# Rows of x in SBUF in bfloat16, DMA transposes in layers 2 to 4, a three-operation feature map and a new PSUM layout in a four-layer linear-attention and MLP kernel

## The chip, the cores and the metric

The kernel runs on one core of one Trainium2 chip. The metric is the device time of one execution in microseconds. A profile is one execution seen by the hardware profiler. TensorE multiplies matrices and writes PSUM; ScalarE (ACT), VectorE (DVE) and GpSimd (POOL) do elementwise work; SyncE (SP) issues DMAs. Each engine works through its own instructions in a fixed order and waits on semaphores for the others.

## What is computed

Four layers stand in a row: attention, MLP, attention, MLP, with the same weights in both turns. S = 2048 rows (tokens) of D = 576, 32 heads of 18, F = 4608. Weights and inputs are bfloat16.

```python
def _A_ref(x, wqkv, wo):                      # H = 32, Dh = 18
    q, k, v = split_heads(x @ wqkv)
    phi = lambda t: jnp.where(t > 0, t + 1, jnp.exp(t)) + 1e-6
    pq, pk = phi(q), phi(k)
    kv = jnp.einsum("bhsd,bhse->bhde", pk, v)
    z = jnp.einsum("bhsd->bhd", pk)
    num = jnp.einsum("bhqd,bhde->bhqe", pq, kv)
    den = jnp.einsum("bhqd,bhd->bhq", pq, z)[..., None] + 1e-6
    return merge_heads(num / den) @ wo

def _B_ref(x, w1, b1, w2, b2):
    y = _layernorm(x, axis=-1)
    h = _gelu(jnp.einsum("bsd,df->bsf", y, w1) + b1)
    return jnp.einsum("bsf,fd->bsd", h, w2) + b2

x = A_x
x = x + _A_ref(_layernorm(x, axis=-1), A_wqkv, A_wo)
x = x + _B_ref(_layernorm(x, axis=-1), B_w1, B_b1, B_w2, B_b2)
x = x + _A_ref(_layernorm(x, axis=-1), A_wqkv, A_wo)
x = x + _B_ref(_layernorm(x, axis=-1), B_w1, B_b1, B_w2, B_b2)
```

## The kernel before

**Tiles.** The 2048 rows are 16 row tiles of 128 and four chunks of 512 (four row tiles each). D = 576 is contracted in five blocks, four of 128 and one of 64. The heads are five groups: four of seven heads (126 columns) and one of four heads (72). The code numbers the layers from 0: layers 0 and 2 are attention ("A"), 1 and 3 the MLP ("B").

**The rows of x between layers** lie in a DRAM tensor `x_d` in float32. `residual` (line 329) adds a finished product in PSUM to the old row tile on VectorE (line 336) and stores the result to `x_d`; `prefetch_xo` (318) loads the old row tile back (in layer 0 from the input), and GpSimd adds the MLP's second bias to it (326). In layer 3 the result goes to the output.

**Layer norm** is a small pipeline, `LNPipe` (216). A row tile is fed to it and moves one stage on at every `tick` (228): a load of x where needed (237), statistics on VectorE (242 to 253), the inverse root by a power on GpSimd (258), the normalised tile into one of four buffers `y_ring` (274: GpSimd for tiles 2 to 15 of layer 0, VectorE mostly; 270: ScalarE for the first four tiles of an MLP), and the transpose: five TensorE transposes into PSUM (287), copied to `yT` by ScalarE (289) or VectorE (291). `yT` holds the transposed, normalised rows of all 16 tiles. In layer 0, `pre_a1_layer0` (642) feeds row tile t+4 and ticks ahead of step t; a tile needs four ticks to its transpose.

**An attention layer** is `layer_A` (344). Its first loop goes over the row tiles: `kv_proj(t)` (350: ten matmuls for k in two halves of 288 columns, ten for v), `kv_acc(t-1)` (375: five matmuls that add the products of v and the mapped k into `kvacc`, which stays in PSUM through the loop), and from t = 4 one `q_proj` (383: five matmuls of 512 columns, for one head group and one chunk). There are 20 of these; those left over are spread over what follows. The feature map `phi_from_psum` (307) is two ScalarE operations that read PSUM (exp, 309; x + 1 + 1e-6, 311) and two on VectorE in bfloat16 in SBUF (min and add, 312; max, 314). Then comes a set-up: the masked `kvacc` to SBUF (408, 412), `z` (418), `kv_wo` (427: kv times wo for a head group), `den_stage` (438: the denominators of a chunk, 20 small matmuls, four more that add 1e-6 by a row `eps_row` times a row of ones, a reciprocal and a masked copy on VectorE) and `scale_stage` (456: the reciprocal spread over a head group by one matmul, a ScalarE copy, and a product into the mapped q; the product is VectorE's, but GpSimd's for the last head group of chunks 1 to 3, 461 and 462). Then the output stage goes over the 16 row tiles: `wo_stage` (465, ten matmuls), its residual, the next chunk's `scale_stage`s, left-over `q_proj`s and `den_stage`s. In it the first four tiles are fed to the next MLP's norm.

**An MLP layer** is `LayerB` (521). For each chunk it runs nine groups of `m1_group` (529: four blocks of 128 hidden units, in pairs of matmuls of 64 rows that run side by side; ScalarE evicts with Gelu, 565; small ScalarE copies, 574, pass the turn on a PSUM bank), then for each row tile of the chunk the second matmul, 72 matmuls of 288 columns (616), and its residual. Meanwhile the next chunk's rows are fed to the norm (`feed_next`, 594), and in layer 1 the finished row tiles for layer 2.

**Order.** `pe` (136) chains TensorE's instructions into program order where it is on: in both MLP layers, in layer 2, and in layer 0 from row tile 8. Elsewhere, and on the other engines, the framework's scheduler orders by priority (program order) and by when it estimates that an instruction is ready. `chained` (128) keeps the loads in order on SP's queue.

**PSUM** has eight banks: three single ones (`ps_h`: k, q, z, den, rden, and two of four blocks of an MLP group), one for transposes (`ps_tp`), and two pairs (`ps_acc`, tags accA and accB: kvacc, v, kv_wo, wo, MLP).

Of the kernel before, what the change touches and what calls it, by code (L numbers as in the profile page):

```python
# [35 lines left out]
def build(tc, A_x, A_wqkv, A_wo, B_w1, B_b1, B_w2, B_b2, out, dbg=None, n_layers=4):  # L36
    nc = tc.nc
    dbg = dbg or {}
    with ExitStack() as ctx:
        const = ctx.enter_context(tc.tile_pool(name="const", bufs=1))  # L40
        ps_h = ctx.enter_context(tc.tile_pool(name="ps_h", bufs=3, space=PSUM))
        ps_tp = ctx.enter_context(tc.tile_pool(name="ps_tp", bufs=1, space=PSUM))
        ps_acc = ctx.enter_context(tc.tile_pool(name="ps_acc", bufs=1, space=PSUM))
        dpool = ctx.enter_context(tc.tile_pool(name="dram", bufs=1, space=DRAM))

        x_in = A_x.flatten_outer_dims()
        out_f = out.flatten_outer_dims()

# [15 lines left out]
        eps_row = const.tile([1, H], BF16, name="eps_row")  # L64
        one_row = const.tile([1, P], BF16, name="one_row")

        def build_masks(after):
            sel = nc.gpsimd.affine_select

            def fill(tile_, value):  # L70
# [10 lines left out]
            fill(eps_row, 1e-6)  # L81
            fill(one_row, 1.0)
# [6 lines left out]
                base=DH - 1, pattern=[[-126, G], [DH, H]], channel_multiplier=-1)  # L89
            fill(quad_mask, 1.0)  # L90
# [10 lines left out]
        wqkv_sb = const.tile([P, KD, 3 * D], BF16, name="wqkv_sb")  # L101
# [5 lines left out]
        b2_bc = const.tile([P, D], BF16, name="b2_bc")  # L107
        yT = const.tile([P, KD, S], BF16, name="yT")
        kvT = const.tile([P, G, 126], BF16, name="kvT")
        zsel = const.tile([P, G, H], BF16, name="zsel")  # L110
        NY = 4
        y_ring = [const.tile([P, DPAD], BF16, name=f"y_ring{i}") for i in range(NY)]
        NV = 3
        v_ring = [const.tile([P, G, P], BF16, name=f"v_ring{i}") for i in range(NV)]
        x_d = dpool.tile([NT, P, D], F32, name="x_d")

        work = ctx.enter_context(tc.tile_pool(name="work", bufs=2))
        blk = ctx.enter_context(tc.tile_pool(name="blk", bufs=NF))

        x0_tiles = {}  # L120

        NOSYNC = mybir.DependencyInfo(mybir.DependencyClass.NoSync, mybir.DependencyReason.SCHED_ONLY)
        SYNC = mybir.DependencyInfo(mybir.DependencyClass.Sync, mybir.DependencyReason.DATA)
        relay_sb = const.tile([P, 2], F32, name="relay_sb")
        nc.gpsimd.memset(relay_sb[:], 0.0)
        chain = dict(last=None)

        def chained(inst):
            if chain["last"] is not None:
                tc.add_manual_dep(inst.ins, chain["last"], NOSYNC, reason="start-up DMA issue order")  # L130
            chain["last"] = inst.ins.name
            return inst

        pe_chain = dict(on=False, last=None)

        def pe(inst):
            if pe_chain["on"]:
                if pe_chain["last"] is not None:
                    tc.add_manual_dep(inst.ins, pe_chain["last"], NOSYNC, reason="TensorE order in the MLP")
                pe_chain["last"] = inst.ins.name  # L140
            return inst

        def load_x0(t):
            x0 = blk.tile([P, D], BF16, name="x0", tag="blk")
            chained(nc.sync.dma_start(out=x0[:], in_=x_in[t * P:(t + 1) * P, :]))
            x0_tiles[t] = x0

        def load_wqkv(part):
            cols = slice(part * D, (part + 1) * D)
            chained(nc.sync.dma_start(out=wqkv_sb[:, 0:4, cols],  # L150
                                      in_=A_wqkv[0:4 * P, cols].rearrange("(k p) n -> p k n", p=P)))
            chained(nc.sync.dma_start(out=wqkv_sb[0:64, 4, cols], in_=A_wqkv[4 * P:D, cols]))

        load_x0(0)
        load_x0(1)
        load_wqkv(1)
        load_x0(2)
        load_x0(3)
        load_wqkv(2)
        load_x0(4)  # L160
        for i in (NY - 1, 0, 1, 2):
            nc.vector.memset(y_ring[i][:], 0.0)
        warm_ps = ps_h.tile([P, 512], F32, name="warm_ps", tag="h")
        for i in range(NWARM):
            nc.tensor.matmul(warm_ps[:], lhsT=y_ring[NY - 1][:, 0:P], rhs=y_ring[NY - 1][:, 0:512], start=True, stop=True)
        act_dummy = const.tile([P, 1], F32, name="act_dummy")
        nc.scalar.activation(out=act_dummy[:, 0:1], in_=neg_half[:, 0:1], func=ACT.Exp)
        nc.vector.memset(wqkv_sb[64:P, 4, :], 0.0)
        for vr in v_ring:
            nc.gpsimd.memset(vr[:, 4, 72:126], 0.0)  # L170
            nc.gpsimd.memset(vr[:, :, 126:127], 1.0)
            nc.gpsimd.memset(vr[:, :, 127:128], 0.0)

        def late_setup():
            build_masks(pool_last["norm"])
# [20 lines left out]
        def piece_b1_dma():  # L196
            b1_raw = work.tile([P, NF], BF16, name="b1_raw", bufs=1)
            with nc.allow_non_contiguous_dma(reason="tiny one-time bias transpose load"):
                chained(nc.sync.dma_start(out=b1_raw[:], in_=B_b1.rearrange("(f p) -> p f", p=P)))
            bias_stage["b1"] = b1_raw  # L200

        def piece_b2_dma():
            chained(nc.sync.dma_start(out=b2_bc[:], in_=B_b2.partition_broadcast(P)))

        def bias_casts():
            nc.vector.tensor_copy(out=b1T[:], in_=bias_stage.pop("b1")[:])

        late_pieces = [piece_wo, piece_b1_dma] + [(lambda i=i: piece_w1(i)) for i in range(9)] + \
                      [(lambda i=i: piece_w2(i)) for i in range(6)]
        late_pads = [late_setup]  # L210

        state = dict(ycnt=0, vcnt=0)
        pool_last = dict(norm=None)
        dve_last = dict(norm=None)

        class LNPipe:
# [3 lines left out]
            def feed(self, xt, t, kind, norm_eng, evac_eng="dve", load_from=None, after=None):  # L220
                self.items.append(dict(stage=(0 if load_from is None else -1), xt=xt, t=t, kind=kind,
                                       norm=norm_eng, evac=evac_eng, load=load_from,
                                       after=after))

            def busy(self):
                return len(self.items)

            def tick(self, transposes=1):
                for it in list(self.items):
                    st = it["stage"]  # L230
                    if st == 4:
                        if transposes == 0:
                            continue
                        transposes -= 1
                    if st == -1:
                        xn = work.tile([P, D], F32, name="xl", tag="xl", bufs=2)
                        nc.sync.dma_start(out=xn[:], in_=x_d[it["load"]])
                        it["xt"] = xn
                    elif st == 0:
                        xt = it["xt"]  # L240
                        stt = work.tile([P, 2, 6], F32, name="ln_st", bufs=4)
                        first = nc.vector.bn_stats(out=stt[:, 0, :], in_=xt[:, 0:HALF])
# [101 lines left out]
        def layer_A(li, next_kind, pre_a1=None):  # L344
# [49 lines left out]
            for t in range(NT):  # L394
                if t == NT // 2:
                    pe_chain["on"] = True
                if pre_a1 is not None:
                    pre_a1(t)
# [329 lines left out]
```

## Time and profile before

| what | us |
|---|---|
| median of 3 runs (lowest, highest) | 809.78 (809.3, 810.58) |
| the profiled execution, span | 809.3 |
| layer 0: to the end of the k/v loop, then set-up, then output stage | 74.6, 13.45, 35.89 |
| layer 1 (MLP) | 289.26 |
| layer 2: k/v loop, set-up, output stage | 55.49, 13.43, 38.26 |
| layer 3 (MLP) | 285.32 |
| after the last matmul | 3.60 |

The stages are cut where TensorE starts the first instruction of the next one. The granted TensorE clock was 0.996 over the span. These are the groups of instructions for the transposes, the feature map and the output stage (line, engine, operation, output and inputs, count, then busy time in us, mean ns of one, idle time of the engine just before them and what ended it):

```profile
L287 PE MATMUL tp<-ident,y_ring 128*128 128x128 bf16 x320 | 29.2, 223 | 3.5 <-DVE y_ring L274 2.5 <-POOL y_ring L274 0.6 <-POOL ln_rstd L258 0.3
L289 ACT COPY yT<-tp 128x640 bf16<-128x640 bf16 x24 | 16.7, 695 | 7.6 <-PE tp L287 7.6
L311 ACT ACTIVATE phi_a<-q_ps 126x512 bf16<-126x512 f32 (+1 forms) x40 | 23.7, 592 | 0.0
L336 DVE TENSOR_TENSOR xn<-m_ps,xo 128x576 f32<-128x576 f32 x16 | 12.1, 758 | 59.5 <-PE m_ps L616 59.5
L470 PE MATMUL wo_ps<-kvwo,pq 126*128 126x288 bf16 (+1 forms) x320 | 48.2, 298 | 13.5 <-POOL pq L462 10.2 <-DVE xn L336 2.1 <-ACT kvwo L434 0.5
```

Matmuls are pipelined, so a mean of one (223 ns for a transpose) is longer than the distance from one to the next.

### The profile page before, as it was taken

The numbers are of one execution on the slowest core, as the hardware profiler recorded it, in microseconds if no ns is written. First come the engines' busy times: TensorE is split into PE (matmuls) and PEld (weight loads), VectorE is DVE, ScalarE is ACT, GpSimd is POOL, SyncE is SP. The second block draws the span as 40 slices with busy tenths as digits, with TensorE's granted clock in tenths as the row PEclk, the third lists the DMA queues.
The fourth block names the chain that finished last, engine by engine and source line by source line (L and its number), as shares of the span: only waits on it lengthen the run. The fifth ranks groups of instructions, "written<-read, shape, count | busy, mean of one in ns | idle before, by whom it ended". The sixth has DMA issues, their size and how long they took to land.

```text
span 809.3 us, 16072 instructions
## 1 busy us (share of the span) xinstructions
PE 783.0 (97%) x6802; PEld 509.1 (63%) x6808; DVE 256.4 (32%) x714; ACT 348.8 (43%) x762; POOL 133.8 (17%) x186
## 2 busy tenths in 40 slices
PE   7999879999999999999999998899999999999998
PEld 4777554486468548745887765546854874685476
DVE  6775881034123403300344467431300300010000
ACT  4778745601630460065037786263047007404610
POOL 6981240012102201100100002120210110011000
PEclk9999999999999999999999999999999999999999
DMA  8991383011112200200110007711300120011000
GB/s 198 260 322 34 97 268 99 2 59 59 31 33 73 72 2 30 74 17 1 60 59 1 1 10 231 260 59 31 95 23 2 52 67 1 2 50 40 2 23 23
DMA packets 43649, 57.07 MB, mean 71 GB/s; under 512 B 10298, under 2 KB 28218, under 8 KB 43578
## 3 DMA queue, kind: packets, MB, share of 16 engines
q1 hardware_dynamic: 43578, 56.06, 22.9%
q8 instruction: 53, 0.87, 0.4%
q14 instruction: 18, 0.15, 0.1%
HBM read 39.53 MB, written 16.52 MB: 69 GB/s over the span
## 4 chain that ended last, share of the span: by engine, by line
PE 87%; POOL 4%; ACT 3%; DVE 2%; DMA 2%; issue 2%; SPq 0%; POOLq 0%; ACTq 0%; DVEq 0%
PE m_ps L616 35%; PE h_ps L569 19%; PE hp_ps L569 15%; PE q_ps L386 4%; PE k_ps L356 4%; PE wo_ps L470 3%; PE v_ps L367 2%; PE tp L287 2%; PE v_ps L364 2%; POOL y_ring L274 2%; ACT rden_bc L460 1%; PE kvacc L380 1%; POOL ln_rstd L258 1%; DMA wqkv_sb<-in_A_wqkv_dram 1%; DVE xn L336 1%
## 5 line engine op out<-in xcount | busy, mean ns | idle before, releaser
L616 PE MATMUL m_ps<-w_sb,hT 128*128 128x288 bf16 x2304 | 289.8, 286 | 0.0
L616 PEld LDWEIGHTS <-hT 128*128 128x128 bf16 x2304 | 223.2, 98 | 57.9 <-issue 3.4
L569 PEld LDWEIGHTS <-w_sb 64*128 64x128 bf16 x2304 | 124.5, 94 | 136.4 <-issue 1.9
L569 PE MATMUL hp_ps<-yT,w_sb 64*128 64x512 bf16 x1152 | 178.0, 376 | 0.0
L574 ACT COPY relay_sb<-relay_sb 128x1 f32<-128x1 f32 x144 | 28.5, 198 | 281.8 <-PE h_ps L569 239.2
L569 PE MATMUL h_ps<-yT,w_sb 64*128 64x512 bf16 x1152 | 147.9, 376 | 0.0
L565 ACT ACTIVATE hT<-h_ps,b1T 128x512 bf16<-128x512 f32 x144 | 91.0, 683 | 44.2 <-PE h_ps L569 44.2
L291 DVE COPY yT<-tp 128x640 bf16<-128x640 bf16 x40 | 19.6, 489 | 262.5 <-PE tp L287 262.5
L565 ACT ACTIVATE hT<-hp_ps,b1T 128x512 bf16<-128x512 f32 x144 | 91.1, 692 | 0.0
L258 POOL TENSOR_TENSOR ln_rstd<-ln_u,neg_half 128x1 f32<-128x1 f32 x64 | 35.5, 554 | 326.4 <-DVE ln_u L251 180.0
L326 POOL TENSOR_TENSOR xo<-xo,b_bc 128x576 f32<-128x576 f32 x32 | 40.9, 1278 | 181.9 <-DMA xo<-x_d 171.2
L470 PE MATMUL wo_ps<-kvwo,pq 126*128 126x288 bf16 (+1 forms) x320 | 48.2, 298 | 13.5 <-POOL pq L462 10.2
L569 PE MATMUL h_ps<-yT,w_tail 64*128 64x512 bf16 x144 | 54.1, 376 | 0.0
L569 PE MATMUL hp_ps<-yT,w_tail 64*128 64x512 bf16 x144 | 54.1, 376 | 0.0
L386 PE MATMUL q_ps<-yT,wqkv_sb 128*126 128x512 bf16 (+1 forms) x200 | 50.0, 382 | 0.5 <-ACT phi_a L311 0.5
L336 DVE TENSOR_TENSOR xbf<-m_ps,xo 128x576 bf16<-128x576 f32 x16 | 12.0, 752 | 117.4 <-PE m_ps L616 117.4
L470 PEld LDWEIGHTS <-pq 126*128 126x128 bf16 (+1 forms) x320 | 31.4, 101 | 27.9 <-POOL pq L462 11.7
L356 PE MATMUL k_ps<-wqkv_sb,yT 128*128 128x288 bf16 x320 | 45.7, 291 | 0.0
L309 ACT ACTIVATE phi_e<-k_ps 128x288 bf16<-128x288 f32 x64 | 27.2, 426 | 36.7 <-PE k_ps L356 36.7
L312 DVE TENSOR_SCALAR phi_e<-phi_e 128x288 bf16<-128x288 bf16 (+2 forms) x104 | 30.8, 297 | 31.1 <-ACT phi_e L309 30.9
L569 PEld LDWEIGHTS <-w_tail 64*128 64x128 bf16 x288 | 27.1, 94 | 17.1
L356 PEld LDWEIGHTS <-yT 128*128 128x128 bf16 x320 | 31.0, 99 | 9.3
(94 smaller groups left out, 656.0 us busy)
## 6 DMA issues: line engine op xcount, KB each, us to landing
x_d<-xn SPq DMA_DIRECT2D x48, 288.0 KB, 2.6
xo<-x_d SPq DMA_DIRECT2D x48, 288.0 KB, 3.0
xl<-x_d SPq DMA_DIRECT2D x24, 288.0 KB, 3.1
w_sb<-in_B_w_dram SPq DMA_DIRECT2D x6, 864.0 KB, 11.5
w_sb<-in_B_w_dram SPq DMA_DIRECT2D x9, 512.0 KB, 5.1
x<-in_A_x_dram SPq DMA_DIRECT2D x17, 144.0 KB, 5.3
xbf<-in_A_x_dram SPq DMA_DIRECT2D x16, 144.0 KB, 3.8
out_dram<-xbf SPq DMA_DIRECT2D x16, 144.0 KB, 1.7
```

The lines of the kernel that those rows point to most:

```text
L258: nc.gpsimd.tensor_tensor(out=rstd[:], in0=it["u"][:], in1=neg_half[:], op=ALU.pow)
L309: act_last["exp"] = nc.scalar.activation(out=e[0:rows, 0:n], in_=ps_ap, func=ACT.Exp).ins.name
L312: nc.vector.tensor_scalar(out=e[0:rows, 0:n], in0=e[0:rows, 0:n], scalar1=1.0, scalar2=1e-6, op0=ALU.min, op1=ALU.add)
L326: nc.gpsimd.tensor_tensor(out=xo[:], in0=xo[:], in1=b2_bc[:], op=ALU.add)
L336: nc.vector.tensor_tensor(out=xn[:].rearrange("p (h n) -> p h n", h=2), in0=halves, in1=xo[:].rearrange("p (h n) -> p h n", h=2), op=ALU.add)
L356: pe(nc.tensor.matmul(kp[:, 0:HALF], lhsT=yT[:, k, tok], rhs=wqkv_sb[:, k, D + half * HALF: D + (half + 1) * HALF], start=(k == 0), stop=( ...
L386: pe(nc.tensor.matmul(qp[0:GR[g], :], lhsT=wqkv_sb[:, k, GO[g]:GO[g] + GR[g]], rhs=yT[:, k, c * CA:(c + 1) * CA], start=(k == 0), stop=(k ...
L470: pe(nc.tensor.matmul(wp[:, half, 0:HALF], lhsT=pq[(g, c)][0:GR[g], j * P:(j + 1) * P], rhs=kvwo[g][0:GR[g], half * HALF:(half + 1) * HALF ...
L565: act_last["gelu"] = nc.scalar.activation(out=hT[f][:, 0:CB], in_=dst[n], func=ACT.Gelu_apprx_tanh, bias=b1T[:, f:f + 1], scale=1.0).ins.name
L569: mm = pe(nc.tensor.matmul(dst[n], lhsT=wt, rhs=mv, start=(seen[n] == 0), stop=(seen[n] == 8)))
L574: relay = nc.scalar.copy(out=relay_sb[:, 1:2], in_=relay_sb[:, 0:1])
L616: pe(nc.tensor.matmul(acc[:, half, 0:HALF], lhsT=hT[f][:, j * P:(j + 1) * P], rhs=w2_sb[:, f, half * HALF:(half + 1) * HALF], start=(f == ...
```

## The change

- **x in SBUF.** `x_sb` holds all rows in bfloat16. `x_d` and its stores and loads go; the input is loaded once, `residual` adds in place, and `bias_rows` makes x + b2 on GpSimd.
- **Norm.** `LNPipe` becomes `Norm`, with the steps `stats`, `rstd`, `norm` and `transposed`, and `Queue`, which takes every fed tile one step on at each tick. For layers 1 to 3 the transpose is a DMA from SBUF to SBUF on SP's queue. In layer 0 it stays on TensorE with a ScalarE copy; it is issued at the end of step t for row tile t+1.
- **Feature map.** exp on ScalarE, min and add on VectorE, then one VectorE operation that reads PSUM: max(x, 0) plus the former. For k all 576 columns go at once. The copy x + 1 on ScalarE goes.
- **PSUM.** Three pairs and two single banks. q, z, den, rden and layer 0's transposes share the two single banks; k, v, kvacc, kv_wo, wo and the MLP's second matmul share the pairs; the MLP's groups use two pairs, or one pair and the two single banks, in turn.
- **The small term 1e-6.** The weights of q lie in groups padded with zeros to 128 columns, so row 126 of a mapped q is one; `zsel` has 1e-6 there, and the four extra matmuls of `den_stage` go.
- **The rest.** All products of `scale_stage` are VectorE's. `pe` chains TensorE throughout. There are two buffers for v instead of three. The masks are built at row tile 8 of layer 0. The weights of q are loaded in ten DMAs, and b1 and b2 after w1.

```diff
-        ps_h = ctx.enter_context(tc.tile_pool(name="ps_h", bufs=3, space=PSUM))
-        ps_tp = ctx.enter_context(tc.tile_pool(name="ps_tp", bufs=1, space=PSUM))
-        ps_acc = ctx.enter_context(tc.tile_pool(name="ps_acc", bufs=1, space=PSUM))
-        dpool = ctx.enter_context(tc.tile_pool(name="dram", bufs=1, space=DRAM))
+        ps_pair = ctx.enter_context(tc.tile_pool(name="ps_pair", bufs=3, space=PSUM))
+        ps_one = ctx.enter_context(tc.tile_pool(name="ps_one", bufs=2, space=PSUM))
...
+            fill(zsel, 0.0)
+            sel(out=zsel[:, 0, :], in_=zsel[:, 0, :], compare_op=ALU.not_equal, fill=1e-6,
+                base=-126, pattern=[[0, H]], channel_multiplier=1)
...
+        def load_wq(k):
+            rows = P if k < 4 else 64
+            src = A_wqkv[k * P:k * P + rows, :]
+            chained(nc.sync.dma_start(out=wq_sb[0:rows, k, 0:4, 0:126],
+                                      in_=src[:, 0:504].rearrange("p (g c) -> p g c", g=4)))
+            chained(nc.sync.dma_start(out=wq_sb[0:rows, k, 4, 0:72], in_=src[:, 504:576]))
...
+            def transposed(self):
+                tok = slice(self.t * P, (self.t + 1) * P)
+                if self.transpose == "dma":
+                    nc.sync.dma_start_transpose(out=yT[:, :, tok], in_=self.y[:])
+                else:
+                    tp = ps_one.tile([P, KD, P], BF16, name="tp", tag="one")
+                    for k in range(KD):
+                        pe(nc.tensor.transpose(out=tp[:, k, :], in_=self.y[:, k * P:(k + 1) * P], identity=ident[:]))
+                    if self.transpose == "act":
+                        nc.scalar.copy(out=yT[:, :, tok], in_=tp[:])
+                    else:
+                        nc.vector.tensor_copy(out=yT[:, :, tok], in_=tp[:])
...
+            def feed(self, t, kind, eng="dve"):
+                n = Norm(t, kind, eng, "dma")
+                self.items.append([n.stats, n.rstd, n.norm, n.transposed])
...
+        def phi(ps_ap, e_ap, out_ap):
+            last["exp"] = nc.scalar.activation(out=e_ap, in_=ps_ap, func=ACT.Exp).ins.name
+            nc.vector.tensor_scalar(out=e_ap, in0=e_ap, scalar1=1.0, scalar2=1e-6, op0=ALU.min, op1=ALU.add)
+            nc.vector.scalar_tensor_tensor(out=out_ap, in0=ps_ap, scalar=0.0, in1=e_ap, op0=ALU.max, op1=ALU.add)
...
+        def bias_rows(t):
+            xo = work.tile([P, D], F32, name="xo", bufs=2)
+            nc.gpsimd.tensor_tensor(out=xo[:], in0=x_sb[:, t, :], in1=b2_bc[:], op=ALU.add)
+            xo_of[t] = xo
...
         def residual(li, t, halves):
+            xo = xo_of.pop(t)[:] if t in xo_of else x_sb[:, t, :]
+            nc.vector.tensor_tensor(out=two(x_sb[:, t, :]), in0=halves, in1=two(xo), op=ALU.add)
+            if li == n_layers - 1:
+                nc.sync.dma_start(out=out_f[t * P:(t + 1) * P, :], in_=x_sb[:, t, :])
...
             for t in range(NT):
+                before_tile(t)
+                k_proj(t)
+                v_proj(t)
                 if t >= 1:
                     kv_acc(t - 1)
                 if t >= 4:
                     q_proj(*q_left.pop(0))
+                if t + 1 in transposes:
+                    transposes[t + 1]()
...
-                eng = nc.gpsimd if c > 0 and g == G - 1 else nc.vector
-                eng.tensor_tensor(out=pq[(g, c)][0:GR[g], 0:CA], in0=pq[(g, c)][0:GR[g], 0:CA],
+                nc.vector.tensor_tensor(out=pq[(g, c)][0:GR[g], 0:CA], in0=pq[(g, c)][0:GR[g], 0:CA],
                                         in1=rb[0:GR[g], 0:CA], op=ALU.mult)
...
+                early = pair("h_ps")
+                if self.turn % 2 == 0:
+                    late = pair("hl_ps")
+                    dst = [early[:, 0, :], late[:, 0, :], early[:, 1, :], late[:, 1, :]]
+                else:
+                    late = [one("h1_ps") for _ in range(2)]
+                    dst = [early[:, 0, :], late[0][:], early[:, 1, :], late[1][:]]
+                self.turn += 1
...
+        norms[0].norm()
+        norms[0].transposed()
+        norms[1].norm()
+        for t in (2, 3):
+            norms[t].stats()
+            norms[t].rstd()
+        norms[1].transposed()
+        norms[2].norm()
...
+        def before_tile0(t):
+            if t + 6 < NT:
+                load_x(t + 6)
+            if t + 4 < NT:
+                norms[t + 4].stats()
+                norms[t + 4].rstd()
+            if t + 3 < NT:
+                norms[t + 3].norm()
+            for _ in range(2 if t % 3 == 2 else 1):
+                if t >= 2 and late_pieces:
+                    late_pieces.pop(0)()
+            if t == 8:
+                build_masks(last["pool_norm"])
...
+                layer_A(li, nk, before_last, {t: norms[t].transposed for t in range(2, NT)})
+            elif kind == "A":
+                layer_A(li, nk, lambda t: lnq.tick(), {})
```

## The prediction

> **What bounds the kernel now.** I read the page's first part, then the chain of waits in order of time, then TensorE's timeline (start, duration, engine, line, operation, what ended idle time before it) of each stage with ScalarE's and VectorE's beside it. TensorE fills the span, so only what shortens its list or its waits counts.
>
> ```profile
> PE 783.0 (97%) x6802; PEld 509.1 (63%) x6808; DVE 256.4 (32%) x714; ACT 348.8 (43%) x762; POOL 133.8 (17%) x186
> ```
>
> In the chain, one chunk's second matmul of layer 3 runs from 698.66 to 735.16, 36.50 us; the last chunk's, in which nothing is transposed, takes 35.40:
>
> ```profile
> 698.66 1.82 PE m_ps L616 x14
> 735.16 1.18 PE h_ps L569 x9
> 770.24 35.40 PE m_ps L616 x288
> ```
>
> Four row tiles are transposed in the former, so one tile (five transposes) costs TensorE 1.10 / 4 = 0.275 us. In layer 0 the step for row tile t is k, v, kvacc, q, and a transpose, back to back; ScalarE's lines lie under TensorE's:
>
> ```profile
> 27.11 1.27 PE L386 MATMUL q_ps<-yT,wqkv_sb 128*126 128x512 bf16 x5
> 28.21 0.44 PE L287 MATMUL tp<-ident,y_ring 128*128 128x128 bf16 x5
> 28.49 1.39 PE L356 MATMUL k_ps<-wqkv_sb,yT 128*128 128x288 bf16 x10
> ...
> 28.41 0.60 ACT L309 ACTIVATE phi_e<-q_ps 126x512 bf16<-126x512 f32 x1 [0.79 <-PE q_ps L386]
> 28.91 0.59 ACT L311 ACTIVATE phi_a<-q_ps 126x512 bf16<-126x512 f32 x1
> 29.39 0.70 ACT L289 COPY yT<-tp 128x640 bf16<-128x640 bf16 x1
> ```
>
> The k projection at 28.49 does not wait for the copy at 29.39: the tile transposed at 28.21 is needed one step later. The step is 4.09 us (24.40 to 28.49). After the k/v loop of layer 2, TensorE passes a set-up (q projections, kv_wo, denominators) and the output stage:
>
> ```profile
> 468.69 2.35 PE L386 MATMUL q_ps<-yT,wqkv_sb 128*126 128x512 bf16 x10
> 482.12 1.44 PE L470 MATMUL wo_ps<-kvwo,pq 126*128 126x288 bf16 x10 [0.24 <-ACT kvwo L434]
> 493.98 0.91 PE L470 MATMUL wo_ps<-kvwo,pq 72*128 72x288 bf16 x6 [1.91 <-POOL pq L462]
> 514.17 6.27 PE L470 MATMUL wo_ps<-kvwo,pq 72*128 72x288 bf16 x36 [2.44 <-POOL pq L462]
> 520.38 1.04 PE L569 MATMUL h_ps<-yT,w_sb 64*128 64x512 bf16 x8
> ```
>
> There it waits for GpSimd's scaling of the fifth head group: six waits, 10.2 us in the two layers.
>
> **Price of the edits, in the order of the run.** Waits between engines, from the same timelines: TensorE's last issue to a ScalarE or VectorE start 0.2 us (kvacc 468.43, ACT v_ring 468.63), VectorE's end to TensorE 0.06.
>
> *Transposes by DMA.* 48 of 64 tiles leave TensorE: 40 in layers 1 and 3 and at the start of layer 2, 40 x 0.275 = 11.0 us; 8 lie in the output stages (below). VectorE's copies of yT go too, off the path. The new DMAs sit on SP's queue, which loses the reads and writes of x_d, behind the weight loads in layer 0 and before the output stores in layer 3. No DMA transpose is in the trace; the nearest rows are the 144 KB store (1.7 us) and the 864 KB load (11.5). Near the smaller (160 KB), I take 3 us. A chunk of 70.5 us has eight, and the last is issued some 20 us before its tile is read, so all are hidden up to about 8.8 us each. The Trainium skill, VectorE: DVE Perf Modes, section The three transpose paths, speaks against the change: 1309 ns by DMA for 128x128 against 390 by TensorE. Five blocks would be an estimated 6.5 us, more than I take, still hidden; TensorE's 0.275 us for five here is far below that page's price, as they are pipelined.
>
> *Layer 0's transposes moved.* They are now issued at the end of step t for the tile that k of step t+1 reads, and the TensorE order is fixed. So k waits for the exp of q (ScalarE 28.41, next free at 28.91) and the yT copy (0.70), to about 29.67: 1.46 us after the transpose's start, of which 0.28 is work, so 1.18 idle. Steps 5 to 15: 11 x 1.18 = 13.0. Before q joins, the v copy is in front instead: copy from 0.75 to 1.42 after v's end, k at 1.47, idle 1.47 - 0.27 - 0.28 = 0.92, three times, 2.8. Against 15.8 stand today's stalls: k(1) to k(15) takes 14.56 to 71.91 = 57.35 where the steps sum to 3 x 3.0 + 11 x 4.09 = 54.0, so 3.4. The loop grows by 12.4; bounds 9.5 (the exp does not get in front: 14 x 0.95 - 3.4) and 15. The start holds two terms that I cancel: k(0) earlier by up to 2 (norm of tile 1 now precedes the statistics of tile 2, which waited 2.04 for x), k(1) later by up to 2 (below). q's weights come in rows of 252 B, 2880 packets for 576; the 4608 packets of b1 moved nearly nothing from 15 to 21 us, about 6 us for 288 an engine, so 180 an engine cost 4 to 5 us for 2: cover is six tiles of x already queued.
>
> *Feature map and PSUM.* ScalarE loses the identity (429 and 592 ns); VectorE gets a max-and-add from PSUM. Nearest is the residual, 752 ns for 128x576 from PSUM, so 0.75 for k and 0.68 for q. A k buffer is held 0.2 + 0.65 (exp of 576) + 0.03 + 0.41 + 0.75 + 0.06 = 2.10 us; with kvacc holding one of three pairs, k and v share two. With q in the step, v + kvacc + q = 1.23 + 0.27 + 1.09 = 2.59 covers it. In layer 2's first four steps only v (and kvacc) does: 2.10 - 1.23 = 0.87, then 3 x 0.60: +2.7 (0 to 3.5). Layer 0's same steps already wait for yT.
>
> *Set-up, two single banks instead of three.* q holds its bank 0.2 + 0.6 + 0.03 + 0.39 + 0.68 + 0.06, about 1.9 us (before 1.3, to the end of phi_a), and z, den and rden take banks from the same two. Walked through in program order from the end of the last q of the loop (469.78): second q after kvacc +0.6, z +0.6, next q +0.8, q behind den +1.2 (the reciprocal, 0.95, holds one bank), first rden +1.2, later rden and q +1.7: 6.1 us idle on 10.3 of work, 16.4, against 12.34 (to 482.12). That is +4.1 a layer, +8.2; bounds 0 (banks free in time) and 11.
>
> *Output stage.* Work is 16 x 1.235 + 15 x 0.216 + 2 x 1.08 + 2 x 0.40 = 26.0 us; the row of ones takes 0.17 off each den, counted here and above. VectorE takes over GpSimd's product (0.44 for 1.16) but has its residuals (0.67 apart), products, reciprocals and statistics of four tiles: 11.3 us in the first four steps against TensorE's 8.6. So about 1.6 for two banks and 1.9 at the first chunk's end; at the two later ends the chain rden, copy 0.58, product 0.42 leaves 0.8 each; 0.6 for the table load (1.28) and the four ScalarE norms (0.87). Sum 31.7, say 31.9. Today 35.9 (88.05 to 123.94) and 38.3: -4.0 and -6.4, -10.4 together; bounds -18 (near TensorE's pace) and -5.
>
> *Others at nothing:* x in SBUF (its DMAs lie under matmuls), the first matmul's PSUM layout (a group of 3.88 us waits for no bank today), the end (3.6 us after the last matmul).
>
> **Sum:** -11.0 + 12.4 + 2.7 + 8.2 - 10.4 = +1.9, so 811.2 for a profiled 809.3; the median shown, 809.78, is 0.48 above that span: **811.7 us**. Its own range is 806 to 818.
>
> **The rivals.**
> 1. *The two single banks do not bind (faster).* If the set-ups keep today's 12.3 us, 811.7 - 8.2 = 803.5. For: VectorE is busy only 9.55 of the 13.43 us of that stage now. Against: q's hold grows on the engine that also does the reciprocals. It decides from 3.5 us of the 8.2 on, where the time passes below 808.2.
> 2. *VectorE stands behind late rows of x at the start (slower).* VectorE waited 3.8 us for x at 14.35 with the feature map of k(0) queued behind. With q's small packets ahead of tile 6 this repeats for two or three tiles, 2 x 3.8 = 7.6: 819. Against: DMA moves 305 to 347 GB/s then, enough for six tiles and k, v weights by 10 us.
> 3. *DMA transposes above 8.8 us each (slower).* At 12 us, eight take 96 us for a chunk of 70.5: 25 us for each of six chunks with successors, over 900. No row near it.
> 4. *Layer 0's new order costs nothing,* because copies start at once and something covers them: 811.7 - 12.4 = 799.3. Against: nothing stands between the transpose and k.
>
> **Chances.** Forecast 0.50 (split by its range: 0.10 faster, 0.12 same, 0.28 slower), rival 1 0.24, rival 2 0.21, rival 3 0.03, rival 4 0.02. Faster 0.36, within 0.2% (about what a measurement of this kernel tells from no change) 0.12, slower 0.52. Range 802 to 821: rivals 1 and 2 inside, 3 and 4 left out.
>
> **What would show it.** Steps of layer 0 from t = 5 at 5.27 us, idle before k put down to ScalarE's yT; second matmuls of 35.4 us in every chunk; k_ps waiting for VectorE at layer 2's start; set-ups of 16.4; output stages near 32 with no GpSimd wait. Wrong if layer 0's step stays at 4.1 or TensorE waits for a DMA of yT.

## The result and the profile after

The changed kernel takes 891.96 us (median of 4 runs, 890.31 to 892.6) beside 809.69 us for the kernel before (4 runs): a ratio of 1.101, 95% interval 1.0998 to 1.103. It is 82.3 us slower where 1.9 were forecast. The profiled execution spans 890.4 us; against the 809.3 before, the traces have 81.1 us to explain.

The head of the page and TensorE's busy line, kernel after:

```profile
span 890.4 us, 15188 instructions
PE 784.4 (88%) x6536; PEld 506.1 (57%) x6536; DVE 240.8 (27%) x608; ACT 323.5 (36%) x618; POOL 129.6 (15%) x190
```

TensorE is as busy as before (784 us for 783) with fewer instructions; what grew is the time in which it stands. The view of waits (engine, what it was to write, what released it: us in all, times, longest) says behind what:

```profile
PE h_ps L146 <- ACT hT L517: 55.9, 72, 0.8
PE k_ps L146 <- ACT yT L273: 9.9, 10, 1.0
PE q_ps L146 <- DVE pq L304: 4.6, 6, 1.1
PE k_ps L146 <- DVE pk L304: 4.2, 4, 2.5
```

Line 146 is the helper through which every matmul now goes, so the tile names tell the places apart. The first line is the largest by far: 72 waits, one in each of the 72 groups of the MLP's first matmul, for ScalarE's Gelu (line 517). Before, TensorE never waited for a Gelu. The group of instructions (busy us, mean ns | idle before it, its releaser) puts all of it on matmuls with the weights `w_tail`, the last of a block:

```profile
L146 PE MATMUL h_ps<-yT,w_tail 64*128 64x512 bf16 x216 | 81.0, 375 | 55.9 <-ACT hT L517 55.9
```

TensorE's timeline over one group of layer 1 (start, duration, engine, line, operation, idle time before and its releaser):

```profile
232.49 1.04 PE L146 MATMUL h_ps<-yT,w_sb 64*128 64x512 bf16 x8
234.31 0.37 PE L146 MATMUL h_ps<-yT,w_tail 64*128 64x512 bf16 x1 [0.78 <-ACT hT L517]
...
239.14 0.37 PE L146 MATMUL h_ps<-yT,w_tail 64*128 64x512 bf16 x1 [0.78 <-ACT hT L517]
```

and ScalarE's over the same:

```profile
233.57 0.69 ACT L517 ACTIVATE hT<-h_ps,b1T 128x512 bf16<-128x512 f32 x1 [0.62 <-PE h_ps L146]
```

The same matmul in the kernel before, in two groups of layer 1, waits for nothing:

```profile
271.57 0.38 PE L569 MATMUL h_ps<-yT,w_tail 64*128 64x512 bf16 x1
275.46 0.38 PE L569 MATMUL h_ps<-yT,w_tail 64*128 64x512 bf16 x1
```

The Gelu of block 0 runs from 233.57 to 234.26; the last matmul of block 2 starts at 234.31, when it has ended. From one such matmul to the next are 239.14 - 234.31 = 4.83 us; before, they were 275.46 - 271.57 = 3.89 (3.88 between others). With 0.96 us for each of the 72 groups, that is 72 x 0.96 = 69 us. The idle time shown, 0.78 us, is shorter than that, as it counts only from the modelled end of the matmul in front.

The other places, on TensorE's timeline: layer 0's step, then the set-up and output stage of layer 2.

```profile
29.39 1.24 PE L146 MATMUL q_ps<-yT,wq_sb 128*128 128x512 bf16 x5
30.47 0.44 PE L271 MATMUL tp<-ident,y_ring 128*128 128x128 bf16 x5
31.90 1.40 PE L146 MATMUL k_ps<-wkv_sb,yT 128*128 128x288 bf16 x10 [0.99 <-ACT yT L273]
...
514.70 2.32 PE L146 MATMUL q_ps<-yT,wq_sb 128*128 128x512 bf16 x10
523.85 1.24 PE L146 MATMUL q_ps<-yT,wq_sb 128*128 128x512 bf16 x5 [1.48 <-DVE rden L418]
532.93 1.40 PE L146 MATMUL wo_ps<-kvwo,pq 126*128 126x288 bf16 x10
543.61 0.47 PE L146 MATMUL den_ps<-pq,zsel 127*32 127x128 bf16 x20 [1.95 <-DVE pq L304]
557.12 1.15 PE L146 MATMUL wo_ps<-kvwo,pq 72*128 72x288 bf16 x6 [1.94 <-DVE pq L429]
570.52 1.04 PE L146 MATMUL h_ps<-yT,w_sb 64*128 64x512 bf16 x8
```

In layer 0 the transpose at 30.47 is now followed at once by the k that needs it, and k waits 0.99 us for the copy. In layer 2 the set-up (first q of the pair at 514.70 to the first wo at 532.93) takes 18.23 us where the kernel before took 482.12 - 468.69 = 13.43, and the output stage (to 570.52) takes 37.59 where it took 38.26. The windows give, for the set-up from the end of the q pair and for the output stage, the length and the busy us of PE, PEld, DVE, ACT and POOL, then clock, DMA share and GB/s:

```profile
515.78:532.93 17.15, 11.38 (x96) 5.82 (x95) 10.93 (x25) 8.81 (x16) 0.00 (x0) 1.00 0.00 1
532.93:570.52 37.59, 30.70 (x227) 19.62 (x226) 33.12 (x83) 14.88 (x25) 11.03 (x24) 0.91 0.16 36
```

In the output stage VectorE works 33.12 of the 37.59 us (26.54 of 38.26 before): GpSimd's waits of before (10.2 us in the two layers) are gone, and waits for VectorE stand there. In the set-up VectorE is not full (10.93 of 17.15 us), but TensorE's longest waits there are for VectorE to finish with a single bank, as at 523.85. The DMA transposes do what they should; the chain of waits gives the second matmul of a chunk of layer 1, during which three tiles are transposed by DMA, and of the last chunk, during which none are:

```profile
343.61 35.38 PE m_ps L146 x288
...
851.32 35.40 PE m_ps L146 x288
```

By layers, the start of one to the start of the next on TensorE:

| stage | before | after | difference |
|---|---|---|---|
| start and layer 0 | 123.94 | 141.84 | +17.9 |
| layer 1 (MLP) | 289.26 | 316.03 | +26.8 |
| layer 2 | 107.18 | 112.65 | +5.5 |
| layer 3 (MLP) and end | 288.9 | 319.9 | +31.0 |

### The profile page after: what moved, and what is told of

The parts are those of the page before. It is cut to its first block, busy times and chain, and to the rows that moved or that the text cites. A ratio compares the mean times of both kernels' runs of the same rounds, so it can differ in the third digit from the quotient of the medians.

```text
span 890.4 us, 15188 instructions
## 1 busy us (share of the span) xinstructions
PE 784.4 (88%) x6536; PEld 506.1 (57%) x6536; DVE 240.8 (27%) x608; ACT 323.5 (36%) x618; POOL 129.6 (15%) x190
## 4 chain that ended last, share of the span: by engine, by line
PE 80%; ACT 9%; DVE 7%; issue 2%; DMA 1%; SPq 1%; POOL 0%; DVEq 0%; POOLq 0%
PE m_ps L146 32%; PE h_ps L146 26%; PE hl_ps L146 7%; ACT hT L517 6%; PE k_ps L146 4%; PE q_ps L146 4%; PE v_ps L146 3%; PE wo_ps L146 2%; ACT phi_e L302 1%; DVE pq L429 1%; DVE ln_st L229 1%; DVE x_sb L318 1%; ACT yT L273 1%; DVE pq L304 1%; DMA wkv_sb<-in_A_wqkv_dram 1%
## 5 line engine op out<-in xcount | busy, mean ns | idle before, releaser
L146 PE MATMUL h_ps<-yT,w_sb 64*128 64x512 bf16 x1728 | 221.6, 376 | 0.0
L517 ACT ACTIVATE hT<-h_ps,b1T 128x512 bf16<-128x512 f32 x216 | 144.5, 686 | 84.8 <-PE h_ps L146 84.8
L313 POOL TENSOR_TENSOR xo<-x_sb,b_bc 128x576 f32<-128x576 bf16 x32 | 40.9, 1279 | 653.7 <-DVE x_sb L318 653.7
L146 PE MATMUL hl_ps<-yT,w_sb 64*128 64x512 bf16 x576 | 88.3, 376 | 0.0
L146 PEld LDWEIGHTS <-yT 128*128 128x128 bf16 x640 | 61.4, 98 | 39.1 <-ACT yT L273 16.1
L146 PE MATMUL k_ps<-wkv_sb,yT 128*128 128x288 bf16 x320 | 44.5, 286 | 16.5 <-ACT yT L273 9.9
L146 PE MATMUL q_ps<-yT,wq_sb 128*128 128x512 bf16 x200 | 49.3, 378 | 8.0 <-DVE pq L304 4.6
L229 DVE BATCH_NORM_STATS2 ln_st<-x_sb 128x6 f32<-128x288 bf16 x128 | 53.2, 440 | 7.4 <-DMA x_sb<-in_A_x_dram 6.7
L517 ACT ACTIVATE hT<-hl_ps,b1T 128x512 bf16<-128x512 f32 x72 | 45.6, 684 | 7.0 <-PE hl_ps L146 7.0
L146 PE MATMUL v_ps<-wkv_sb,yT 128*128 128x252 bf16 (+1 forms) x320 | 44.4, 285 | 3.3 <-DMA wkv_sb<-in_A_wqkv_dram 1.7
## 6 DMA issues: line engine op xcount, KB each, us to landing
w_sb<-in_B_w_dram SPq DMA_DIRECT2D x6, 864.0 KB, 10.4
```

The lines of the kernel that those rows point to most:

```text
L146: return pe(nc.tensor.matmul(out_, lhsT=lhsT, rhs=rhs, start=start, stop=stop, **kw))
L229: ins = nc.vector.bn_stats(out=stt[:, h, :], in_=xt[:, h * HALF:(h + 1) * HALF])
L313: nc.gpsimd.tensor_tensor(out=xo[:], in0=x_sb[:, t, :], in1=b2_bc[:], op=ALU.add)
L517: last["gelu"] = nc.scalar.activation(out=hT[f][:, 0:CB], in_=dst[n], func=ACT.Gelu_apprx_tanh, bias=b1T[:, f:f + 1], scale=1.0).ins.name
```

## The experiments

### Where the 69 us come from

In the changed kernel each group takes one two-bank tile for blocks 0 and 2. The built program's list of TensorE instructions (number, line, operation, output and inputs, what it waits for) has, in each of the 72 groups, a wait for ScalarE at the last matmul of block 2:

```
1998 L146 Matmult h_ps<-yT,w_sb 128x512
2000 L146 Matmult h_ps<-yT,w_tail 128x512 [waits Activation_49]
2002 L146 Matmult h_ps<-yT,w_sb 128x512
```

Block 0's last matmul is the first of the three lines, and its Gelu is issued between it and the second; it is this Gelu that the second waits for. The theory: a two-bank tile is one thing for the program's dependencies, so a matmul into one of its banks waits for a Gelu that reads the other, if that Gelu was issued before. Two experiments test it from both ends. The first keeps the changed layout and issues the Gelu of block 0 only after block 2's last matmul:

```diff
-                    if seen[n] == 9 and n != 3:
+                    if seen[n] == 9 and n in (1, 2):
+                        if n == 2:
+                            evict(0)
                         evict(n)
```

> The changed kernel with one edit: in each MLP group the Gelu of block 0 is issued after block 2's last matmul instead of before it. Theory (blocks 0 and 2 now lie in one PSUM tile of two banks, and the last matmul of block 2 is made to wait for the Gelu that reads block 0): the 0.78 us wait in each of 72 groups goes, a group falls from 4.84 to about 3.88 us, 72 x 0.96 = 69 us, so about 822 us. Rival (the banks of a pair disturb each other, or ScalarE is late with its turn-passing copies): a group stays near 4.8 and the time near 890.

Measured 825.18 us (819.03 to 828.21), ratio to the kernel before 1.019 (1.015 to 1.023); 66.8 us less than the changed kernel. TensorE waits for no Gelu any more, and the group is back at 238.11 - 234.23 = 3.88 us (TensorE's timeline, this experiment, last matmul of block 2 in one group and the next):

```profile
234.23 0.38 PE L146 MATMUL h_ps<-yT,w_tail 64*128 64x512 bf16 x1
...
238.11 0.38 PE L146 MATMUL h_ps<-yT,w_tail 64*128 64x512 bf16 x1
```

The second puts the pairing alone into the kernel before:

```diff
-                dst = [hps[0][:], pair[:, 0, :], hps[1][:], pair[:, 1, :]]
+                dst = [pair[:, 0, :], hps[0][:], pair[:, 1, :], hps[1][:]]
```

> The kernel before with one edit: in each MLP group blocks 0 and 2 lie in the two-bank pair and blocks 1 and 3 in the single banks (it was the other way round). Theory (sharing of one tile by blocks 0 and 2): the wait appears here too, 72 x about 0.96 us, so about 879 us with a group near 4.84 us. Rival (the slow groups come from the three pairs and two singles as a whole, or from another part of the change): the time stays near 810.

Measured 880.25 us (878.9 to 881.12), ratio 1.086 (1.084 to 1.088), and the same line in its view of waits:

```profile
PE hp_ps L569 <- ACT hT L565: 55.9, 72, 0.8
```

One line that swaps which two blocks share a tile costs 70 us in a kernel otherwise unchanged. Before, blocks 1 and 3 shared it; block 3's Gelu is held until the next group, and by the time block 1's is issued no matmul of block 3 is left.

### Layer 0's order

This experiment adds one edit to the late Gelu of the first: the next tile's transposes are issued before k of step t instead of after q:

```diff
                 before_tile(t)
+                if t + 1 in transposes:
+                    transposes[t + 1]()
                 k_proj(t)
...
-                if t + 1 in transposes:
-                    transposes[t + 1]()
```

> As the first run of this call, and the TensorE transposes of layer 0 are issued ahead of k of step t for row tile t+1, one whole step earlier than in the changed kernel. Theory (the 0.99 us wait of k for ScalarE's yT copy is layer 0's loss): steps from t = 5 fall from 5.24 to about 4.1 us, 11 x 1.13 + 3 x 0.8 = 14 to 15 us less than the first run, about 808 us. Rival (the steps are held by the maps of q and k instead): the steps stay above 4.8 and less than 5 us are gained.

Measured 809.06 us (807.51 to 812.04, 10 runs), ratio 0.9991 (0.9976 to 1.0006). From step 5 on the step is 34.46 - 30.39 = 4.07 us, and these k wait for nothing (but for one, 0.27 us), although the copy of the tile just transposed starts later than k (0.69 us from 34.88 on ScalarE), as it is for the next step:

```profile
30.11 0.44 PE L271 MATMUL tp<-ident,y_ring 128*128 128x128 bf16 x5
30.39 1.39 PE L146 MATMUL k_ps<-wkv_sb,yT 128*128 128x288 bf16 x10
...
34.18 0.44 PE L271 MATMUL tp<-ident,y_ring 128*128 128x128 bf16 x5
34.46 1.39 PE L146 MATMUL k_ps<-wkv_sb,yT 128*128 128x288 bf16 x10
```

In the two traces the stretch up to the loop's last q shrinks from 85.97 to 73.94 us, 12.0. The medians differ by 16.1, but the four runs of the first experiment lie 9 us apart, so the trace gives the better size. With these two mends the changed kernel is level with the one before.

### The transposes by DMA alone

The kernel before, with the transposes of layers 1 to 3 by DMA and nothing else changed:

```diff
+                        if it["dma"]:
+                            nc.sync.dma_start_transpose(out=yT[:, :, t * P:(t + 1) * P], in_=y[:])
+                            self.items.remove(it)
+                            continue
                         tp = ps_tp.tile([P, KD, P], BF16, name="tp", tag="tp")
```

> The kernel before with one part of the change alone: the transposes of layers 1 to 3 go by DMA. Theory (they cost TensorE 0.275 us a tile and a DMA of 2.4 us hides): 48 x 0.275 = 13 us less, about 796.5 us, second matmuls of 35.4 us in all chunks. Rival (DMAs queued behind the stores and loads of x, so that a later row tile waits): no gain, 808 us or more.

Measured 795.77 us (794.73 to 800.68), ratio 0.983 (0.980 to 0.986). It is the part of the change that pays: 14.7 us off for 13 expected, and the rival is out. The profile's DMA issues (count, median us from issue to landing), this experiment:

```profile
yT<-y_ring SPq DMA_TRANSPOSE x48, 2.9
```

### Set-up and output stage

The next experiments stand on the kernel with both mends (809.06). This table is read from TensorE's timelines, of one execution each, so a stage can differ by some us from its usual length: set-up from the pair of q projections that ends the loop to the first wo, output stage from there to the MLP, us, layer 0 / layer 2.

| kernel | set-up | output stage |
|---|---|---|
| before | 13.43 / 13.43 | 35.89 / 38.26 |
| before, transposes by DMA | 13.43 / 13.43 | 38.47 / 35.19 |
| changed | 18.23 / 18.23 | 36.64 / 37.59 |
| both mends | 18.23 / 18.23 | 37.77 / 36.61 |
| + statistics held | 18.23 / 20.76 | 34.33 / 34.32 |
| + four-operation map | 15.71 / 15.29 | 36.57 / 35.30 |
| + den and z in half a pair | 15.42 / 15.42 | 35.94 / 37.00 |
| all three of these | 13.85 / 13.85 | 34.70 / 34.61 |

**Statistics held.** With all of x in SBUF, VectorE's norm statistics of the MLP's tiles 4 to 15 have their input early and can stand in the output stage. Here they wait for attention's last residual (`a_end`):

```diff
+                    if self.kind == "B" and self.t >= TPC:
+                        tc.add_manual_dep(ins.ins, last["a_end"], NOSYNC, reason="after the attention layer's rows")
```

> On the early-transpose version (809.06 us): the statistics of the MLP's row tiles 4 to 15 come on VectorE after the attention layer's last residual. In the changed kernel they stand inside the output stage, because x in SBUF makes them ready there. Theory (they crowd the products and residuals out): 12 tiles x about 0.95 us leave each output stage, which falls from 37.6 to about 32 us; 2 x 5.5 = 11 us, about 798 us. Rival (TensorE waits for banks, not for a full VectorE): less than 3 us.

Measured 807.4 us (803.6 to 808.83), ratio 0.9958 (0.9937 to 0.9978): 1.7 us less, not 11, and hardly clear of the 0.9976 to 1.0006 without this edit. The expectation had counted too many tiles: in VectorE's timeline of the changed kernel, the statistics of only four of the twelve tiles stand in layer 0's output stage and of six in layer 2's. The two output stages do shrink, by 3.4 and 2.3 us, but in the profiled execution layer 2's set-up grows by 2.5. In that set-up the five matmuls of a q projection, 1.24 us elsewhere, take 2.09, and the windows show a granted clock (the third number from the end) of a half or little more:

```profile
480.53 2.09 PE L146 MATMUL q_ps<-yT,wq_sb 128*128 128x512 bf16 x5 [0.21 <-ACT rden_bc L432]
```

```profile
482.00:484.00 2.00, 1.27 (x4) 0.47 (x3) 0.68 (x2) 1.07 (x2) 0.00 (x0) 0.50 0.00 0
...
486.00:488.00 2.00, 2.00 (x9) 1.01 (x8) 0.00 (x0) 0.56 (x2) 0.00 (x0) 0.60 0.00 0
```

So VectorE's load is one part of these stages, the granted clock another; more on that at the end.

**The old feature map.** Four operations with ScalarE as the last reader of PSUM:

```diff
-            nc.vector.scalar_tensor_tensor(out=out_ap, in0=ps_ap, scalar=0.0, in1=e_ap, op0=ALU.max, op1=ALU.add)
+            nc.scalar.activation(out=out_ap, in_=ps_ap, func=ACT.Identity, bias=C1, scale=1.0)
+            nc.vector.tensor_tensor(out=out_ap, in0=out_ap, in1=e_ap, op=ALU.max)
```

> On the early-transpose version (809.06 us): the feature map of four operations again, x + 1 by ScalarE and a maximum in bfloat16, so that ScalarE is the last to read PSUM. Theory (the map that reads PSUM on VectorE holds q's and k's banks longer, 1.9 against 1.3 us for q): the set-up falls from 17.2 to about 14.5 us, layer 2's first steps lose their 0.46 us waits, the output stages gain 1 to 2 each: 8 us in all, about 801 us. Rival (only the count of single banks matters): within 3 us of 809.

Measured 800.34 us (799.39 to 803.6), ratio 0.988 (0.986 to 0.991): 8.7 us less for 8 expected. In the traces the set-ups give 2.5 + 2.9 of it and the output stages 1.2 + 1.3. The three-operation map of the change had moved the last reading of PSUM to VectorE, where it takes 0.69 us for q (0.76 for k), and a bank is free only after it.

**The denominators in half a pair,** so that two single banks serve q and rden alone:

```diff
-                dp = one("den_ps")
+                dp = pair("den_ps")[:, 0, :]
```

(and the same for `zp`.)

> On the early-transpose version (809.06 us): the denominators and z take half of a PSUM pair instead of a single bank. Theory (two single banks shared by q, z, den and rden are what the set-up waits for): its waits for the reciprocal (1.48 and 0.49) and z (0.29 and 0.85) go, and den's wait of 1.96 in the output stage: 3 us a set-up and 1.5 an output stage, 9 us in all, about 800 us. Rival (VectorE is the bound there): less than 3 us.

Measured 805.0 us (803.72 to 808.37), ratio 0.9935 (0.9913 to 0.9957): 4.1 us less for 9 expected. The set-ups shrink by 2.8 each, since no q waits for the reciprocal's bank any more (1.48 us at 523.85 in the changed kernel); of the output stages one shrinks by 1.8 and the other grows by 0.4, for 1.5 less expected in each.

**Both of these,** held statistics and half a pair:

> The two edits of the runs e5 and e7 together. Theory (two separate losses, VectorE's order in the output stage and the two single banks): the gains add up, 809 - 11 - 9, about 789 us, below both the kernel before and the one with DMA transposes alone (795.8). Rival (both free the same wait): no more than the larger of the two.

Measured 802.42 us (801.85 to 806.78), ratio 0.992, where 789 was expected: 6.6 us less than with the two mends. The size was missed as in each alone, but the gains do add (1.7 + 4.1 = 5.8), as the theory said.

**All mends and the old map:**

> The changed kernel with all mends at once: late Gelu of block 0, early transposes in layer 0, statistics held, den and z in half a pair, and the four-operation feature map. Theory (VectorE sets the pace of set-up and output stages, and the feature map's two VectorE operations that read PSUM are the largest part of it): the single gains of the three last edits (1.7, 4.1 and 8.7 us against 809.1) add up for the most part: 795 us (792 to 798), ratio 0.982. Rival (the den/z edit and the map remove the same waits, those for pq of q's eviction): 800 us, no better than the map alone.

Measured 793.0 us (791.34 to 798.02), ratio 0.980 (0.9776 to 0.9825): the theory's 795, not the rival's 800. The gains of the three last edits add up (14.5 us singly, 16.1 together), so they take different waits away, and the set-up is back at 13.85 us. The interval overlaps that of the transposes alone (0.980 to 0.986). Whether anything else of the change helps, x in SBUF among it, is therefore not shown here.

**GpSimd's product.** First in the kernel before with DMA transposes, moved to VectorE; then, in the kernel with all mends, moved back to GpSimd:

```diff
-                eng = nc.gpsimd if c > 0 and g == G - 1 else nc.vector
+                eng = nc.vector
```

> The kernel before with DMA transposes in layers 1 to 3, and the product of the last head group (72x512, 1147 ns on GpSimd, 6 times) on VectorE in every chunk. In the trace of the kernel before with DMA transposes alone, PE waits 6.6 us for GpSimd's products in front of wo's matmuls. Theory (that wait is on the path, and VectorE has room for 0.4 us more per product): 789 us (786 to 792) beside 795.8. Rival (VectorE is full in the output stage, and the product waits there as long): 795, within 2 us of the kernel without this edit.

Measured 797.35 us (796.43 to 797.87), ratio 0.984 (0.9825 to 0.9854): no gain beside 795.77. The rival was right. The wait has changed its name only, as the views of waits (us in all, times, longest) show, with the product on GpSimd:

```profile
PE wo_ps L474 <- POOL pq L466: 6.6, 4, 1.9
```

and on VectorE:

```profile
PE wo_ps L474 <- DVE pq L466: 6.3, 7, 2.0
```

> All mends at once as above, but the product of the last head group on GpSimd for the chunks after the first, as the kernel before has it. Theory (VectorE is the bound of the output stages, so 6 products of 0.4 us less on it help, but each takes about 1.15 us on GpSimd and its wo group waits for it): within 3 us of the kernel with all mends. If VectorE's length were all that counts: 3 us faster; if GpSimd's latency binds as in the kernel before: 3 to 6 us slower.

Measured 794.06 us (792.72 to 794.69), ratio 0.980 (0.978 to 0.981): the same as with the product on VectorE. So where this was tried, GpSimd's waits were not a price that the move to VectorE could save: VectorE is late there as well. The 10.2 us of the kernel before itself were not tried alone; with DMA transposes they are 6.6.

## Why the prediction was wrong

**The step that failed** is the one that put at nothing "the first matmul's PSUM layout (a group of 3.88 us waits for no bank today)". The sentence in brackets is true of the kernel before and says nothing of the one after. The new layout makes other blocks share a tile, and the question that was not asked is which ScalarE operation reads that tile between two of its matmuls. It costs 0.96 us a group, 72 x 0.96 = 69 us, shown from both ends by the first two experiments. Even the size was in the trace of before: the wait is TensorE's end to ScalarE's start 0.2, the Gelu 0.69 and 0.06 back, 0.95 us. The Trainium skill's page Perfetto Trace Analysis, section Matmuls, asks that independent groups of matmuls rotate through different banks, so that the reading of one overlaps the next. Blocks 0 and 2 did use different banks, and the trace shows 0.78 us idle all the same. The Trainium skill's page PSUM — Partial Sum Buffer, section PSUM bank collisions raise a hardware error, quotes that each PSUM bank in each partition is a separate RAM. By that the two would not have collided. Here the wait stands in the program, on one instruction; whether the overlap would have been safe was not tried.

**The other large miss** is a term of the sum: the output stages, put at 31.9 us each, -10.4 together. They took 36.64 and 37.59 where 35.89 and 38.26 were: +0.1. Two things were left out of the 31.9. VectorE's work was undercounted: the prediction counts the statistics of four tiles, where those of eight stand in layer 0's stage and of ten in layer 2's (eight and six before), and VectorE is busy 33 of 37.6 us in the latter. And the sum has no term for the granted clock, which was 0.91 in both (1.00 and 0.91 before). The statistics are only a part: held back, they leave the stages at 34.3 us, still above 31.9. Moving the product off GpSimd gave nothing where tried by itself.

**With both corrected** the sum closes: +1.9 + 69 + 10.5 = +81.4, and the traces differ by 81.1. It closes so well partly by luck: the set-ups grew by 9.6 for 8.2 put, and the k/v loop of layer 2 by 1.3 for 2.7.

**What held:**

- *Transposes by DMA:* put at 3 us each and hidden below 8.8; they landed in 2.4 us (median), and the second matmul of every chunk takes 35.4 us. Alone they give 14.7 us by the medians. The traces show 10.7 of it in the MLP layers and the k/v loop of layer 2, for 11.0 put. The output stages, where 8 x 0.275 = 2.2 were to come off, changed by +2.6 and -3.1. The profiled execution took 800.68 us, 4.9 above its median, so where the rest of the 14.7 lies is not shown. From the 1309 ns of VectorE: DVE Perf Modes of the Trainium skill, section The three transpose paths, the prediction worked out an estimate of 6.5 us for five blocks. The 2.4 us measured are well below it, and decide.

```profile
yT<-y_ring SPq DMA_TRANSPOSE x48, 2.4
```

- *Layer 0's order:* +12.4 put, and the loop's last q comes 86.97 - 74.62 = 12.35 us later. Step 5.23 us for 5.27 put, idle 0.99 for 1.18. That the sum fits so closely is partly luck, as the parts were not quite those put: from step 4 to step 15 it loses 57.57 - 47.51 = 10.1 us; the other 2.3 arise at the start. There, in part, the second rival came true (VectorE behind late rows of x), once and not two or three times (VectorE's timeline, after):

```profile
24.20 0.82 DVE L229 BATCH_NORM_STATS2 ln_st<-x_sb 128x6 f32<-128x288 bf16 x2 [3.04 <-DMA x_sb<-in_A_x_dram]
```

- *Set-ups:* +4.1 each put, +4.8 measured (to 16.4 put from the end of the loop's last q, 17.15 measured); the rival that single banks don't bind is out.
- *Layer 2's first steps:* 0.60 us put on each of three and 0.87 on the first. On TensorE's timelines each of the three is about 0.6 longer, from one k to the next (3.33 us for 2.72, or 2.99 where a transpose stood in the step), and the first is not (2.44 for 2.45). The waits are for VectorE's pk, as said.
- *Feature map:* put at 0.75 us for k and 0.68 for q from the residual's row; measured 0.757 and 0.687.
- The direction, slower, came right by luck, for a reason that was not in the sum.

Two smaller sums of the prediction are off, and nothing hangs on them: the lower bound of layer 0's term, 14 x 0.95 - 3.4, is 9.9 and not 9.5, and 180 packets at 6 us for 288 are 3.75 us and not 4 to 5.

## What to carry to other kernels

When buffers are laid out anew, don't ask whether the old layout waits: write down, for each shared tile, which engine reads it between two of its writes, in program order, and price that chain (here 0.2 + 0.69 + 0.06 us, times 72 groups). Before an edit that hands work to another engine, count that engine in that stage alone; here VectorE was at 27% of the span and at 88% of layer 2's output stage, and taking over GpSimd's product gained nothing. And of a change in many parts, one (here the DMA transposes) can hold nearly all the gain: 14.7 us alone, beside 17.6 for the change with all mends and the old feature map.

## What the runs showed of the hardware

The granted TensorE clock fell to a half after some stretches in which TensorE mostly waited, though no single gap in them was long. In the kernel with all mends, TensorE's timeline in layer 2's output stage:

```profile
486.71 0.53 PE L146 MATMUL wo_ps<-kvwo,pq 126*128 126x288 bf16 x3 [0.89 <-DVE x_sb L321]
487.86 0.30 PE L146 MATMUL wo_ps<-kvwo,pq 126*128 126x288 bf16 x1 [0.62 <-DVE pq L434]
489.98 0.91 PE L146 MATMUL wo_ps<-kvwo,pq 72*128 72x288 bf16 x6 [1.82 <-DVE ln_u L240]
...
491.16 2.47 PE L146 MATMUL wo_ps<-kvwo,pq 126*128 126x288 bf16 x10
```

and its windows of 1 us:

```profile
490.00:491.00 1.00, 1.00 (x8) 0.72 (x9) 0.97 (x4) 0.00 (x0) 0.82 (x2) 1.00 0.09 18
491.00:492.00 1.00, 1.00 (x7) 0.59 (x6) 0.75 (x2) 0.97 (x2) 0.04 (x1) 0.65 0.00 0
492.00:493.00 1.00, 1.00 (x6) 0.64 (x5) 0.54 (x2) 0.85 (x2) 0.90 (x3) 0.50 0.00 0
493.00:494.00 1.00, 1.00 (x5) 0.55 (x4) 0.67 (x2) 0.87 (x1) 0.07 (x1) 0.50 0.67 154
494.00:495.00 1.00, 1.00 (x7) 0.65 (x6) 0.71 (x2) 0.59 (x1) 0.24 (x1) 0.64 0.06 10
```

From 486 to 490 TensorE is busy 0.84 of 4 us, with no single gap above 1.82 us; from about 491.3 to 494.7 the clock is a half, though TensorE works without a pause, and ten wo matmuls take 2.47 us instead of 1.40. The Trainium skill, TensorE: Matmul & The Clock Gate, section Why this matters for your kernels, warns of gaps above about 3 us. Here half clock followed a stretch of smaller ones. The length of a gap alone doesn't tell, though. In the kernel with both mends, k waits 3.22 us in layer 0, and the granted clock stays at 1.00 in the windows around it and after:

```profile
26.33 1.39 PE L146 MATMUL k_ps<-wkv_sb,yT 128*128 128x288 bf16 x10 [3.22 <-DVE pk L304]
```

Such a dip lies in the output stage of layer 2 in the kernel before, too (mean clock 0.91), and in the kernel with held statistics it had moved into layer 2's set-up, while layer 0's set-up of the same execution, with the same instructions and the same waits up to there, took 18.23 us at a clock of 1.00. Work at half clock for 3.4 us is half done, so such a stall takes an estimated 1.7 us on top where TensorE sets the pace, and the time of these stages can jump by some us between kernels whose instructions hardly differ (that set-up: 20.76 us for 18.23). What brings a dip on was not tried by itself, and how much of the stages' remaining 34.6 us is clock and how much VectorE stays open.
